# Reordering the first loads and widening the first six steps of a fused window-attention and feed-forward kernel

## The chip, the core and the metric

The kernel runs on one core of one Trainium2 chip. The metric is the device time of one execution in microseconds; the kernel before takes 308.42 us (median of three runs, 308.12 to 308.52). The profiler's record of one execution spans 306.1 us. The engines are TensorE (PE: matmuls; PEld: its weight loads), VectorE (DVE), ScalarE (ACT), GpSimd (POOL, which here mostly issues loads) and SyncE (SP, which issues the output's stores).

## What is computed

Sliding-window attention over 8 batches, 8 heads, 576 positions and head size 64, where a position sees those up to 32 away, and then a two-layer feed-forward network over the 4608 tokens with a smooth ReLU between the layers:

```python
scores = q @ k.T / sqrt(64); outside |i - j| <= 32: -1e9
x      = softmax(scores) @ v                 # (4608, 512) after the heads are put side by side
h      = x @ w_in                            # w_in  (512, 2048)
g      = h where h >= 1, 0 where h <= -1, (h + 1)**2 / 4 between
out    = g @ w_out                           # w_out (2048, 512)
```

Inputs and output are fp32. The loads cast to bf16 on their way, but for the first half of the first batch's q, which comes as fp32 (`q32`) and is cast on the core. Matmuls take bf16 and sum in fp32.

## The kernel before

**Units of work.** The first layer is cut into slots. Slot `a` is token block `t = a // 8` of 256 tokens and feature block `f = a % 8` of 256 features: eight matmuls of 256 columns into `hp` (128 x 512 fp32, one bank of PSUM). The smooth ReLU of a slot is an ACT step and two DVE steps, or, for the slots in `two_on_act`, two ACT steps and one DVE step:

```python
A.activation(rr, hp, AF.Relu, scale=0.5, bias=0.5)
if a in two_on_act:
    A.activation(mx, rr, AF.Square)
    V.scalar_tensor_tensor(g, hp, 1.0, mx, op0=ALU.max, op1=ALU.min)
else:
    V.tensor_max(mx, hp, rr)
    V.scalar_tensor_tensor(g, rr, 1.0, mx, op0=ALU.min, op1=ALU.mult)
```

Attention of a batch is cut into: `tpose` (q or k is transposed by PE, and copied out of PSUM by ACT and DVE), `scores` (a mask matmul by `add_mask` while slots are below 14, the products, Exp on ACT), `sums` (products with v and with ones into one tile; its `end` takes Ln and Exp on ACT for the reciprocal and puts off a DVE product into `xT`, which `flush()` issues), and `scores8` for the last 96 positions. The rows `kk = 0, 2` of `xT` come from `sums` with `y1 = 0`, and `kk = 1, 3` from `y1 = 1`.

The second layer's first two token blocks go in `pair(x)`: eight matmuls of 256 columns, with `half = x // 8` the half of w_out's columns, `p = x % 8 // 4` the token block, and `x % 4` the group of four of w_out's 16 row groups. They accumulate in a tile of `ps_o`:

```python
pairs = [(6, 0), (7, 1), (8, 2), (9, 3), (11, 4), (12, 5), (15, 6), (15, 8), (16, 7), (17, 9)]   # (slot, pair)
```

**Loads.** GpSimd issues them in this order (`load_half(1, ...)` is the rest of the first batch's q and k, `load_rows(1, ...)` the second batch's q and k):

```python
for h in range(2):
    load_half(0, 1, h)               # k of the first half
load_v(0, 0) ... load_v(0, 3)
cuts = [0, 256, 512, 768, 1024, 1280, 1792, DFF]
w = [(load_w_in, c0, c1, h) for c0, c1 in zip(cuts, cuts[1:]) for h in range(2)]
put(w[:4] + [(load_half, 1, t, h) for t in range(2) for h in range(2)] + w[4:12])
put([(load_w_out, 0, 0, 4)] + w[12:])
put([(load_w_out, 0, k, k + 4) for k in range(4, 16, 4)] + [(load_rows, 1, t) for t in range(2)])
put([(load_v, 1, n) for n in range(4)])
```

**The start.** PSUM has pools `ps_h` (two tiles of one bank), `ps_s` and `ps_n` (one tile of two banks each) and, for the start, `ps_p` (two banks), whose place `ps_o` (two tiles of one bank) takes later. `keep_warm(n, ...)` issues n matmuls on a tile of zeros, whose result is not used.

```python
    ...                                   # q and k of the first half: transposes, copies, scores
    keep_warm(4, ps_h, "hp")
    e0 = sums(0, 0, 0, TB)
    e1 = sums(0, 1, 0, TB, ps_p)
    keep_warm(5, ps_h, "hp")
    e0()
    e1()
```

**The slots.** What is to happen at a slot is in a list by `at`; a slot's matmuls and its smooth ReLU come first, then what `at` holds for it, then its pairs, then what `at` holds for the slot and a half.

```python
at(1, (tposes, 0, (0, 1), (1, 1)))                                      # the rest of q and k
at(2, (scores, 0, (0, 1), (0, 2), (2, 4)), (scores8, 0, ps_o))
at(3, (scores, 0, (1, 2), (0, 2), (2, 4), ps_n), (sums, 0, 0, TB, MAIN, ps_s))
at(4, (sums, 0, 1, TB, MAIN))
at(5, (sums, 0, 0, MAIN, S, ps_s))
at(13, seq[0][1])                                                       # second batch: scores
at(13.5, (*seq[1][1], ps_n))
at(14, (*seq[0][0], ps_s), seq[1][0])                                   # second batch: sums
for t in range(2):
    at(11 + t, (tposes, 1, (t, 0), (t, 1)))                             # second batch: q, then k
```

From slot 18 on the kernel goes on in the same manner, with the loads of later batches well ahead, and none of that is touched by the change.

Of the kernel before, what the change touches and what calls it, by code (L numbers as in the profile page):

```python
# [14 lines left out]
def kernel(  # L15
# [29 lines left out]
    WIDE = 72, 136  # L45
    LONG = 2

    const = ctx.enter_context(tc.tile_pool(name="const", bufs=1))
# [5 lines left out]
    osp = ctx.enter_context(tc.tile_pool(name="osp", bufs=3))  # L54
    ps_h = ctx.enter_context(tc.tile_pool(name="ps_h", bufs=2, space=bass.MemoryType.PSUM))
    ps_s = ctx.enter_context(tc.tile_pool(name="ps_s", bufs=1, space=bass.MemoryType.PSUM))
# [24 lines left out]
    def load_half(half, t, h, eng=None, x=None):  # L81

        src, dst, nm = ((q, qn, "qh"), (k, kn, "kh"))[t]
        if (0, half) not in dst:
            dst[0, half] = early.tile([128, 2, S], BF, name=nm, tag=nm, bufs=2) if x is None else x
        (eng or nc.gpsimd).dma_start(out=dst[0, half][:, h], in_=src[0].rearrange(  # L86
            "(h y) (l p j) d -> h l p y (j d)", h=2, l=2, p=32)[h][half])
# [21 lines left out]

    def load_w_in(c0, c1, h):  # L110
        nc.gpsimd.dma_start(out=w_in[64 * h:64 * h + 64, :, c0:c1],  # L111
                            in_=moe_w_in.rearrange("(h y d) f -> h d y f", h=2, d=64)[h][:, :, c0:c1])

# [33 lines left out]

    cuts = [0, 256, 512, 768, 1024, 1280, 1792, DFF]
    w = [(load_w_in, c0, c1, h) for c0, c1 in zip(cuts, cuts[1:]) for h in range(2)]
    put(w[:4] + [(load_half, 1, t, h) for t in range(2) for h in range(2)] + w[4:12])  # L150
    put([(load_w_out, 0, 0, 4)] + w[12:])
    put([(load_w_out, 0, k, k + 4) for k in range(4, 16, 4)] + [(load_rows, 1, t) for t in range(2)])
    put([(load_v, 1, n) for n in range(4)])
# [85 lines left out]

    def scores8(b, eng, pool=None):  # L240

        p = pt8[b] = ptp.tile([128, 2, 2, TAIL], BF, name="pt8")
        if pool:
            ps = [pool.tile([128, 2 * TAIL], FP, name="s8", tag="op") for h in range(2)]
        else:
            bb = two_banks(ps_s)
            ps = [bb[:, h, :2 * TAIL] for h in range(2)]
        if eng is None:
            add_mask(ps, 2, TAIL)
        for y1 in range(2):  # L250
            for a in range(2):
                for h in range(2):
                    s0 = S * (y1 + 2 * a) + MAIN
                    nc.tensor.matmul(ps[h][HD[a], TAIL * y1:TAIL * y1 + TAIL], kT[b][HD[h], s0 + 32:s0 + TAIL],
                                     qTs[b % 3][HD[h], PAD + s0:PAD + s0 + TAIL],
                                     start=eng is not None, stop=True, skip_group_check=True)
        like = "p h y j -> p h (y j)"
        if pool:
            for h in range(2):
                A.activation(p[:, h].rearrange("p y j -> p (y j)"), ps[h], AF.Exp, scale=D ** -0.5)  # L260
        else:
            A.activation(p.rearrange(like), bb[:, :, :2 * TAIL], AF.Exp, scale=D ** -0.5)
        mask(eng, p, mask8.rearrange("p (h y j) -> p h y j", h=2, y=2))
# [55 lines left out]

    def tp1(pool):  # L320
        if pool is ps_h:
            return pool.tile([128, 8, 128], BF, name="tp", tag="hp")
        return pool.tile([128, 2, 8, 128], BF, name="tp", tag="bb")[:, 0]

    def tposes(b, *sets):

        todo = []
        for (t, half), pool in zip(sets, (ps_s, ps_n)):
            tp = pool.tile([128, 2, 8, 128], BF, name="tp", tag="bb")
            todo += [tpose(b, 2 * half + part, t, (A.copy, V.tensor_copy)[part], tp[:, part]) for part in range(2)]  # L330
        for copy in todo:
            copy()

    def keep_warm(n, pool, tag):

        z = pool.tile([128, 512], FP, name="z", tag=tag)
        for _ in range(n):
            nc.tensor.matmul(z, warm[:, :128], warm, start=True, stop=True)

# [7 lines left out]

    with tc.tile_pool(name="ps_p", bufs=1, space=bass.MemoryType.PSUM) as ps_p:
        keep_warm(11, ps_h, "hp")

# [4 lines left out]
        qn[0, 0] = cast(q32, "qb", 5)  # L355
        qq = [tpose(0, n, 0, (A.copy, V.tensor_copy)[n], tp1(ps_h)) for n in range(2)]
        for x in qq:
            x()
        kk = [tpose(0, n, 1, (A.copy, V.tensor_copy)[n], tp1((ps_n, ps_p)[n])) for n in range(2)]
        keep_warm(1, ps_h, "hp")  # L360
        first = two_banks(ps_s)
        add_mask([first[:, h] for h in range(2)], 4, 128)
        for x in kk:
# [3 lines left out]
        scores(0, (1, 2), (0, 2), (0, 2), None, ps_p)  # L367
        keep_warm(4, ps_h, "hp")
        e0 = sums(0, 0, 0, TB)
        e1 = sums(0, 1, 0, TB, ps_p)  # L370
        keep_warm(5, ps_h, "hp")
        e0()
        e1()
    ps_o = ctx.enter_context(tc.tile_pool(name="ps_o", bufs=2, space=bass.MemoryType.PSUM))

    NB = NT // TB
    NF = DFF // 256  # L380
    pairs = [(6, 0), (7, 1), (8, 2), (9, 3), (11, 4), (12, 5), (15, 6), (15, 8), (16, 7), (17, 9)]
    two_on_act = (1, 7, 8, 9, 10, 11, 12)
    ev = {}
# [12 lines left out]

    at(1, (tposes, 0, (0, 1), (1, 1)))
    at(2, (scores, 0, (0, 1), (0, 2), (2, 4)), (scores8, 0, ps_o))
    at(3, (scores, 0, (1, 2), (0, 2), (2, 4), ps_n), (sums, 0, 0, TB, MAIN, ps_s))
    at(4, (sums, 0, 1, TB, MAIN))  # L400
    at(5, (sums, 0, 0, MAIN, S, ps_s))
    seq = [x for b in range(1, B) for x in steps(b, 224)]
    at(13, seq[0][1])
    at(13.5, (*seq[1][1], ps_n))
    at(14, (*seq[0][0], ps_s), seq[1][0])
# [9 lines left out]
    for t in range(2):  # L415
        at(11 + t, (tposes, 1, (t, 0), (t, 1)))
    loads, xps = {}, {16: [(2, 0)], 18: [(2, 1)]}
# [55 lines left out]
    def run(pos):  # L473
        todo = []
        for fn, *x in ev.get(pos, []):
            if fn is sums:
                todo.append(sums(*x))
            elif fn is tposes:
                tposes(*x)
            else:  # L480
                pool = (x.pop(),) if x[-1] in (ps_s, ps_n, ps_o) else ()
                fn(*x, eng, *pool)
        for end in todo:
            end()

    def project(hp, f, r0, todo, first, last):

        for n, (j, kk) in enumerate(todo):
            nc.tensor.matmul(hp[:, j], w_in[:, kk, 256 * f + 128 * j:256 * f + 128 * j + 128],  # L489
                             xT[:, kk, r0:r0 + TB], start=first and n == 0, stop=last and n == len(todo) - 1,  # L490
                             skip_group_check=True)

    hps = []
    done = 4 * (40 - NF)
    for a in range(NF * NB + 2 * NF):
        wide = WIDE[0] <= a < WIDE[1]
        eng = None if a < 14 else V
        post = [] if a >= 40 else [x for n, x in pairs if n == a] + [a - NF] * (a >= 2 * NF + 2)
        for b, x in loads.get(a, []):
            if x < 2:  # L500
                load_nat(b, x)
            else:
                for n in range(4):
                    load_v(b, n)
        if a == 0 or a > 3:
            flush()
        if a < NF * NB:
            if wide:
# [3 lines left out]
                hp = ps_h.tile([128, 2, TB], FP, name="hp", tag="hp")  # L512
                for n, kk in enumerate((0, 2, 1, 3)):
                    nc.tensor.matmul(hp.rearrange("p n t -> p (n t)"), w_in[:, kk, 128 * f:128 * f + 128],  # L514
                                     xT[:, kk, r0:r0 + 2 * TB], start=n == 0, stop=n == 3)
                g = gT[:, f, home(t):home(t + 1) + 1:home(t + 1) - home(t)]
            else:
                t, f = divmod(a, NF)
                r0 = TB * t % RING
                if a in (0,):  # L520
                    hps = [ps_h.tile([128, 2, TB], FP, name="hp", tag="hp") for _ in range(2)]
                    for y in range(2):
                        for n in range(2):
                            project(hps[n], f + n, r0, [(j, y + 2 * m) for j in range(2) for m in range(2)], y == 0, y == 1)
                elif not hps:
                    pool, tag = (ps_o, "op") if a == 6 else (ps_h, "hp")
                    hps = [pool.tile([128, 2, TB], FP, name="hp", tag=tag)]
                    project(hps[0], f, r0, [(j, kk) for j in range(2) for kk in (0, 2, 1, 3)], True, True)
                hp = hps.pop(0)
                g = gT[:, 2 * f:2 * f + 2, home(t)]  # L530

            rr = ewp.tile([128, 2, TB], FP, name="rr")
            A.activation(rr, hp, AF.Relu, scale=0.5, bias=0.5)  # L533
            mx = ewp.tile([128, 2, TB], FP, name="mx")
            if a in two_on_act:
                A.activation(mx, rr, AF.Square)
                V.scalar_tensor_tensor(g, hp, 1.0, mx, op0=ALU.max, op1=ALU.min)
            else:
                V.tensor_max(mx, hp, rr)  # L539
                V.scalar_tensor_tensor(g, rr, 1.0, mx, op0=ALU.min, op1=ALU.mult)  # L540
        flush()
# [45 lines left out]
```

The softmax here doesn't subtract the row's maximum and nothing guards it: scores larger than these inputs give would overflow.

## Time and profile before

| | before |
|---|---|
| time, median of 3 | 308.42 us |
| span of the profiled execution | 306.1 us |
| granted TensorE clock | 1.00 |
| moved by DMA | 35.67 MB, mean 117 GB/s |
| HBM read, written | 36.70 MB, 9.44 MB |

A line of the timeline reads: start in us, busy us, engine, source line, operation, output <- inputs, shape and count, and in brackets the idle time of the engine before it with what ended it. In the windows view a line has the stretch, its length, and for PE, PEld, DVE, ACT and POOL the busy time and number of instructions, then the granted clock, the busy time of the DMA engines as a share (their packets overlap, so it passes 1), and GB/s. Line 489 is a slot's first-layer matmul, line 464 a pair, line 189 a transpose of q or k, lines 539, 540 and 537 the DVE steps of a slot, and line 307 the product into `xT`.

### The profile page before, as it was taken

The page shows a single profiled execution, that of the slowest core. Times are in us where ns is not written, and L with a number is a line of the kernel's source. Part 1 is how long each engine was busy: PE and PEld are TensorE (multiplying, and loading weights), DVE is VectorE, ACT ScalarE, POOL GpSimd, SP SyncE. Part 2 cuts the span into 40 slices and gives each one's busy share as a digit, 9 for nine tenths or more (in the row PEclk, how much of TensorE's full clock was granted, in tenths as well). Part 3 has the DMA queues.
Part 4 walks back from the last instruction along what each step waited for, and adds up shares of the span by engine and source line. Part 5 has one row for each costly group of instructions (what it writes and reads, how often), then busy time and mean ns, then how long its engine had stood idle before and what let it go on. Part 6 is the DMA issues. An engine that isn't in the chain of part 4 may idle for free.

```text
span 306.1 us, 7974 instructions
## 1 busy us (share of the span) xinstructions
PE 298.4 (97%) x3388; PEld 181.2 (59%) x3388; DVE 239.6 (78%) x376; ACT 191.2 (62%) x320; POOL 77.1 (25%) x92
## 2 busy tenths in 40 slices
PE   8889999999999999999999999999999999999995
PEld 3468878876666676666654544444445444446644
DVE  3268568888888989998999998888888888788700
ACT  3688896748856856776766766665667654444311
POOL 8787661037009009004600900000000000000000
PEclk9999999999999999999999999999999999999999
DMA  9999999999999999999998991550101000000121
GB/s 153 184 197 198 186 196 153 173 156 164 139 186 109 181 169 124 165 144 116 148 127 166 145 156 39 111 115 34 36 34 37 36 34 35 36 34 34 59 80 69
DMA packets 137171, 35.67 MB, mean 117 GB/s; under 512 B 122160, under 2 KB 132912, under 8 KB 137136
## 3 DMA queue, kind: packets, MB, share of 16 engines
q0 software_dynamic: 102976, 18.06, 83.5%
q1 hardware_dynamic: 34016, 16.81, 26.1%
q8 instruction: 26, 0.43, 0.6%
q10 hardware_dynamic: 144, 0.29, 0.3%
q14 instruction: 9, 0.07, 0.1%
HBM read 36.70 MB, written 9.44 MB: 151 GB/s over the span
## 4 chain that ended last, share of the span: by engine, by line
PE 91%; POOL 3%; DMA 2%; ACT 1%; issue 1%; DVE 0%; POOLq 0%; ACTq 0%
PE op L449 36%; PE hp L489 22%; PE hp L514 18%; PE bb L295 6%; PE op L464 4%; PE bb L229 2%; DMA w_in<-in_moe_w_in_dram 2%; POOL vn L107 1%; PE op L440 1%; POOL w_in L111 1%; PE tp L189 1%; ACT pt L237 1%; POOL kh L86 1%; POOL qh L86 0%; PE bb L208 0%
## 5 line engine op out<-in xcount | busy, mean ns | idle before, releaser
L533 ACT ACTIVATE rr<-hp 128x512 f32<-128x512 f32 x144 | 85.5, 595 | 86.1 <-PE hp L514 41.7
L449 PE MATMUL op<-w_out,gT 128*128 128x512 bf16 x496 | 126.9, 380 | 0.0
L539 DVE TENSOR_TENSOR mx<-hp,rr 128x512 f32<-128x512 f32 x137 | 94.4, 689 | 26.1 <-ACT rr L533 24.3
L540 DVE SCALAR_TENSOR_TENSOR gT<-rr,mx 128x512 bf16<-128x512 f32 x137 | 94.8, 692 | 4.7
L489 PE MATMUL hp<-xT,w_in 128*128 128x256 bf16 x640 | 83.1, 273 | 2.2 <-DMA w_in<-in_moe_w_in_dram 1.4
L489 PEld LDWEIGHTS <-w_in 128*128 128x128 bf16 x640 | 61.8, 98 | 22.7 <-issue 2.8
L449 PEld LDWEIGHTS <-gT 128*128 128x128 bf16 x496 | 46.1, 98 | 45.2
L514 PE MATMUL hp<-xT,w_in 128*128 128x512 bf16 x256 | 65.7, 379 | 0.0
L514 PEld LDWEIGHTS <-w_in 128*128 128x128 bf16 x256 | 25.0, 98 | 30.2
L99 POOL DMA_DIRECT2D qn<-in_q_dram x12 | 14.6, 1224 | 89.5 <-DMA kT<-kn 87.4
L237 ACT ACTIVATE pt<-bb 128x1024 bf16<-128x1024 f32 (+1 forms) x33 | 32.7, 1001 | 4.5 <-PE bb L229 3.1
L107 POOL DMA_DIRECT2D vn<-in_v_dram x32 | 27.7, 900 | 4.8 <-DMA w_out<-in_moe_w_out_dram 4.0
L307 DVE TENSOR_TENSOR xT<-bb,rc 128x512 bf16<-128x512 f32 (+1 forms) x32 | 21.0, 657 | 9.6 <-ACT rc L302 8.7
L453 ACT COPY osb<-op 128x512 f32<-128x512 f32 x31 | 18.0, 580 | 11.4 <-PE op L449 11.1
L302 ACT ACTIVATE rc<-lr 128x512 f32<-128x512 f32 (+2 forms) x40 | 23.5, 587 | 1.3
L301 ACT ACTIVATE lr<-bb 128x512 f32<-128x512 f32 (+2 forms) x40 | 22.1, 552 | 0.3 <-PE bb L295 0.3
L203 DVE TENSOR_TENSOR pt<-pt,mask 128x1024 bf16<-128x1024 bf16 (+1 forms) x33 | 20.3, 614 | 0.5 <-ACT pt L237 0.5
L295 PE MATMUL bb<-pt,ones 64*64 64x256 bf16 (+3 forms) x352 | 19.6, 255 | 0.1
L295 PE MATMUL bb<-pt,vn 64*64 64x128 bf16 (+3 forms) x712 | 18.4, 204 | 0.1
L295 PEld LDWEIGHTS <-ones 64*64 64x64 bf16 x352 | 10.3, 105 | 11.6 <-issue 11.6
L295 PEld LDWEIGHTS <-vn 64*64 64x64 bf16 x712 | 16.7, 107 | 0.3 <-DMA vn<-in_v_dram 0.3
L464 PE MATMUL op<-w_out,gT 128*128 128x256 bf16 x128 | 16.5, 273 | 0.0
(61 smaller groups left out, 140.3 us busy)
## 6 DMA issues: line engine op xcount, KB each, us to landing
out_dram<-osb SPq DMA_DIRECT2D x35, 256.0 KB, 2.3
vn<-in_v_dram POOLq DMA_DIRECT2D x32, 144.0 KB, 9.7
qn<-in_q_dram POOLq DMA_DIRECT2D x12, 288.0 KB, 6.2
kn<-in_k_dram POOLq DMA_DIRECT2D x12, 288.0 KB, 9.0
w_in<-in_moe_w_in_dram POOLq DMA_DIRECT2D x12, 128.0 KB, 5.6
w_out<-in_moe_w_out_dram POOLq DMA_DIRECT2D x4, 256.0 KB, 8.0
w_out<-in_moe_w_out_dram POOLq DMA_DIRECT2D x2, 512.0 KB, 13.2
kh<-in_k_dram POOLq DMA_DIRECT2D x4, 144.0 KB, 5.4
```

The lines of the kernel that those rows point to most:

```text
L107: nc.gpsimd.dma_start(out=vn[b][64 * a:64 * a + 64, :, h], in_=v[b, y:y + 2].rearrange("y s d -> (y s) d") .rearrange("(c r) d -> r c d", ...
L237: A.activation(p, ps[:, :, :w * n].rearrange(like, y=m), AF.Exp, scale=D ** -0.5)
L295: nc.tensor.matmul(bb[HD[h], a, o + c0:o + c1], ones[HD[a]] if c is None else vn[b][HD[a], c, h], p(a, h), start=n == 0, stop=True, skip_g ...
L301: A.activation(lr[:, :, :D0], bb[:, :, D0:2 * D0], AF.Ln)
L302: A.activation(rc[:, :, :D0], lr[:, :, :D0], AF.Exp, scale=-1.0)
L449: nc.tensor.matmul(op[tt], gT[:, j, home(tt // 2), 128 * (tt % 2):128 * (tt % 2) + 128], w_out[:, j], start=j == 0, stop=j == 15)
L464: nc.tensor.matmul(o[:, tt], gT[:, j, p, 128 * tt:128 * tt + 128], w_out[:, j, 256 * half:256 * half + 256], start=not done, stop=len(done ...
L489: nc.tensor.matmul(hp[:, j], w_in[:, kk, 256 * f + 128 * j:256 * f + 128 * j + 128], xT[:, kk, r0:r0 + TB], start=first and n == 0, stop=l ...
L514: nc.tensor.matmul(hp.rearrange("p n t -> p (n t)"), w_in[:, kk, 128 * f:128 * f + 128], xT[:, kk, r0:r0 + 2 * TB], start=n == 0, stop=n == 3)
L533: A.activation(rr, hp, AF.Relu, scale=0.5, bias=0.5)
L539: V.tensor_max(mx, hp, rr)
L540: V.scalar_tensor_tensor(g, rr, 1.0, mx, op0=ALU.min, op1=ALU.mult)
```

## The change

It does five things. The rest of the first batch's q and k is loaded ahead of w_in. w_in comes in pieces of 512 columns and of every second row group `kk` (0 and 2, or 1 and 3), each in two halves of the partitions, where it came in pieces of 256 columns and all row groups. The first batch's whole attention is done by the start section, woven between slots 0 to 5, which are now three `double` steps: two slots in one tile of two banks, whose ReLU steps have 1024 columns. The second batch's q and k are loaded ahead of half of w_out's first columns, and transposed at slots 10 and 11, between the slot's ACT steps and its DVE step. And the pairs, the choice of `two_on_act` and the PSUM tiles of slots 6 to 8 are set anew. It is for fewer waits of TensorE at the start. The core of the diff:

```diff
-    cuts = [0, 256, 512, 768, 1024, 1280, 1792, DFF]
-    w = [(load_w_in, c0, c1, h) for c0, c1 in zip(cuts, cuts[1:]) for h in range(2)]
-    put(w[:4] + [(load_half, 1, t, h) for t in range(2) for h in range(2)] + w[4:12])
-    put([(load_w_out, 0, 0, 4)] + w[12:])
-    put([(load_w_out, 0, k, k + 4) for k in range(4, 16, 4)] + [(load_rows, 1, t) for t in range(2)])
+    put([(load_half, 1, t, h) for t in range(2) for h in range(2)])
+    put([(load_w_in, c, e, h) for c in range(0, DFF, 512) for e in range(2) for h in range(2)])
+    put([(load_w_out, 0, k, k + 4) for k in (0, 4)] + [(load_rows, 1, t) for t in range(2)])
+    put([(load_w_out, 0, k, k + 4) for k in (8, 12)])
 ...
+    def smelu(hp, g, rr, mx, two_on_act, mid=None):
+        A.activation(rr, hp, AF.Relu, scale=0.5, bias=0.5)
+        if two_on_act:
+            A.activation(mx, rr, AF.Square)
+            flush()
+            if mid:
+                mid()
+            V.scalar_tensor_tensor(g, hp, 1.0, mx, op0=ALU.max, op1=ALU.min)
+        else:
+            flush()
+            V.tensor_max(mx, hp, rr)
+            V.scalar_tensor_tensor(g, rr, 1.0, mx, op0=ALU.min, op1=ALU.mult)
 ...
+    def double(n, pool, between=None):
+        hp = pool.tile([128, 2, 2, TB], FP, name="hp4", tag="bb")
+        for kk in KK:                                            # 0, 2, 1, 3
+            for f in range(2):
+                project(hp[:, f], 2 * n + f, 0, [(j, kk) for j in range(2)], kk == KK[0], kk == KK[-1])
+            if kk == KK[1] and between:
+                between()
+        smelu(hp.rearrange("p n j t -> p (n j t)"), gT[:, 4 * n:4 * n + 4, 0], rr4[n % 2], mx4, False)
 ...
-        keep_warm(5, ps_h, "hp")
+        tp = tp2(ps_e)
+        qq = [tpose(0, 2 + n, 0, (V.tensor_copy, A.copy)[n], tp[:, n]) for n in range(2)]
         e0()
+        flush()
+        qq[0]()
         e1()
+        flush()
+        qq[1]()
+        keep_warm(3, ps_n)
+        tp = tp2(ps_s)
+        kk = [tpose(0, 2 + n, 1, (V.tensor_copy, A.copy)[n], tp[:, n]) for n in range(2)]
+        rest = two_banks(ps_n)
+        add_mask([rest[:, h] for h in range(2)], 4, 128)
+        for x in kk:
+            x()
+        scores(0, (0, 1), (0, 2), (2, 4), None, ready=rest)
+        double(0, ps_e, lambda: scores(0, (1, 2), (0, 2), (2, 4), None))
+        sums(0, 0, TB, MAIN)()
+        scores8(0, None)
+        double(1, ps_p)
+        sums(0, 1, TB, MAIN, ps_s)()
+        double(2, ps_e, lambda: sums(0, 0, MAIN, S)())
 ...
-    pairs = [(6, 0), (7, 1), (8, 2), (9, 3), (11, 4), (12, 5), (15, 6), (15, 8), (16, 7), (17, 9)]
-    two_on_act = (1, 7, 8, 9, 10, 11, 12)
+    pairs = [(8, 0), (9, 1), (11, 4), (12, 2), (13, 5), (14, 3), (15, 6), (15, 8), (16, 7), (17, 9)]
+    two_on_act = (6, 7, 8, 9, 10, 11, 12)
 ...
-    at(13, seq[0][1])
-    at(13.5, (*seq[1][1], ps_n))
+    at(12.5, seq[0][1])
+    at(13, (*seq[1][1], ps_n))
 ...
-        at(11 + t, (tposes, 1, (t, 0), (t, 1)))
+        at(10.25 + t, (tposes, 1, (t, 0), (t, 1)))
 ...
+                if a == 8:
+                    hp = two_banks(ps_s)[:, 0].rearrange("p (j t) -> p j t", j=2)
+                else:
+                    pool, tag = (ps_o, "op") if a < 8 else (ps_h, "hp")
+                    hp = pool.tile([128, 2, TB], FP, name="hp", tag=tag)
+            smelu(hp, g, rr, mx, a in two_on_act, lambda: run(a + 0.25))
```

At the start `ps_e` (two banks) takes the place of `ps_h`, which is opened after it, together with `ps_o`.

## The prediction

> **What bounds the kernel now.** I read the page first, then the windows view cut at the points where the work changes, then TensorE's waits, then the timelines of the first 45 us. The page:
>
> ```profile
> span 306.1 us, 7974 instructions
> PE 298.4 (97%) x3388; PEld 181.2 (59%) x3388; DVE 239.6 (78%) x376; ACT 191.2 (62%) x320; POOL 77.1 (25%) x92
> ```
>
> TensorE (PE) is busy 97% of the span; nothing else is over 78%. Where the other 3% lie is told by the windows view (busy time in each stretch):
>
> ```profile
> 0.00:11.60 11.60, 10.11 (x152) 5.24 (x153) 3.34 (x16) 5.80 (x8) 10.26 (x20) 1.00 1.50 158
> 11.60:33.60 22.00, 19.29 (x301) 15.08 (x299) 14.85 (x23) 17.35 (x32) 17.31 (x25) 1.00 1.34 199
> 33.60:44.80 11.20, 11.05 (x216) 8.87 (x216) 6.95 (x11) 9.88 (x16) 7.11 (x7) 1.00 1.83 189
> 44.80:302.80 258.00, 257.93 (x2726) 152.05 (x2724) 214.45 (x327) 157.84 (x266) 42.39 (x42) 1.00 1.05 105
> ```
>
> The second number is the length, the third PE's busy time. After 44.8 us PE has 0.07 us of idle time in 258 us, and the change leaves that work alone. So the whole effect must show before that point, which is the first-layer product of slot 15. The change can move the end only by the time at which PE finishes slot 15. What could be won is the idle time from 11.6 to 44.8 us, 2.71 + 0.15 = 2.9 us, some 0.2 us more for each wait (a matmul's recorded end is later than the next one's issue: 8 of them start 0.87 us apart, the last ends at 1.04), and the filler matmuls on `warm`: 4 to 5 us, 1.5% of the span. A gain of 2% is out of reach. PE's timeline names the waits:
>
> ```profile
> 13.24 0.60 PE L489 MATMUL hp<-xT,w_in 128*128 128x256 bf16 x4 [0.44 <-DVE xT L307]
> 14.50 1.47 PE L489 MATMUL hp<-xT,w_in 128*128 128x256 bf16 x12 [0.67 <-DMA w_in<-in_moe_w_in_dram]
> ...
> 17.12 0.69 PE L189 MATMUL tp<-ident,kh 128*64 128x128 bf16 x17 [0.47 <-DMA kh<-in_k_dram]
> 18.53 1.03 PE L489 MATMUL hp<-xT,w_in 128*128 128x256 bf16 x8 [0.72 <-DMA w_in<-in_moe_w_in_dram]
> 33.59 1.03 PE L489 MATMUL hp<-xT,w_in 128*128 128x256 bf16 x8 [0.33 <-DVE gT L537]
> ```
>
> Three are for loads. DVE's timeline shows the other engine that matters; here it works off slots 4 and 5 without a gap, and ends only at 27.9 us:
>
> ```profile
> 24.68 0.68 DVE L539 TENSOR_TENSOR mx<-hp,rr 128x512 f32<-128x512 f32 x1
> 25.39 0.69 DVE L540 SCALAR_TENSOR_TENSOR gT<-rr,mx 128x512 bf16<-128x512 f32 x1
> 26.00 0.62 DVE L307 TENSOR_TENSOR xT<-bb,rc 128x448 bf16<-128x448 f32 x1
> 26.54 0.68 DVE L539 TENSOR_TENSOR mx<-hp,rr 128x512 f32<-128x512 f32 x1
> 27.25 0.69 DVE L540 SCALAR_TENSOR_TENSOR gT<-rr,mx 128x512 bf16<-128x512 f32 x1
> ```
>
> [...]the trace has 688 for line 539. [...]2 x 0.61 when two of 512 follow each other without a gap (29.04 to 29.65). [...]before, w_in's packets are 512 B, mostly, and move 192 to 198 KB/us, q and k at 1152 B some 204, v at 128 B 135 to 162. Packets of 1024 B will thus gain a few per cent at most. [...]the granted clock is 1.00 in every window.
>
> **The change part by part, loads first.** The page's DMA row is 9 in all early slices: loads come at the rate of the DMA engines, so order is all. A landing is an issue (GpSimd timeline) plus the time to landing (DMA view). Before: the fourth piece of v at 10.6, the fourth of w_in 14.4, the last k half 17.1, and from there 128 KB of w_in each 0.65 us. After, the q and k halves (144 KB, 0.7 us each) follow v: 11.4, 12.1, 12.85 and, with half a microsecond for the slow spot near 13 us, 13.9. w_in comes then in 16 pieces of 128 KB. By the same sum of bytes the first 512 columns are complete at 17.1, their even row groups at 15.75; the later quarters at 19.75, 22.45, 25.15. Then w_out's first two quarters 26.5 and 27.85, q and k of the second batch 30.8 and 33.7 (before: 33.3 and 36.2), w_out's others 35.1 and 36.5.
>
> **Then PE's new order,** with issue times from the timeline: 8 matmuls of 256 columns 0.875, an 18-transpose half of q or k 0.56, mask and scores 0.34 + 0.22, sums 0.42 to 0.53; 0.2 from the last issue to ACT's start, 0.05 from DVE to PE. In the instruction order of the built kernel a second copy out of a shared transpose tile waits for the first, on the other engine; I keep that.
>
> The sums end at 11.54 as before. q's transposes wait for 12.2 (0.66 lost), the fillers for DVE's product until 13.23 (0.47), k's for 14.0 (0.13); the mask ends 14.9. k's copies, DVE 0.75 then ACT 0.65, end at 15.97: scores at 16.02 (1.12 lost). Slots 0 and 1 are multiplied 16.24 to 18.56, with scores between. ACT: Exp to 18.95, 1024-column Relu (estimated 1.03 from the Exp of that width) to 19.9. On PE the sums and tail scores follow, slots 2 and 3 to 20.97, a wait of 0.5 for the tail's Exp, sums, slots 4 and 5 to 24.32.
>
> DVE now begins its first slot at 19.9, against 16.2 before, and from there it is full: six steps of 1024 at 1.24, two products of 0.62 and one of 0.55 make 9.2 less overlap, so to 28.85; slot 6's step ends 29.5. PE waits 0.7 for the last quarter of w_in, does slots 6, 7, 8 to 27.66, and then meets the first pair. That needs an accumulator from the pool `ps_o` of two buffers, and slots 6 and 7 hold both. It waits for slot 6's step: 29.53, 1.87 lost. Then pair 0, slot 9, pair 1, slot 10 to 33.03, q's 36 transposes, slot 11 to 35.02. k's transposes follow with nothing between but slot 11, and share q's two buffers: they wait for q's copies on ACT and DVE until 35.97 and 36.65 (1.07 lost; before, a pair and a slot lay between). Pair 4, slot 12, pair 2, scores, slot 13, scores, pair 5, slot 14, sums, pair 3, slot 15: 9.3 us with no wait, to 46.5.
>
> Sum: 0.66 + 0.47 + 0.13 + 1.12 + 0.5 + 0.14 + 0.7 + 1.87 + 1.07 = 6.7 us lost where the kernel before loses 4 to 5, two fillers saved included. Slot 15 ends at 46.5 instead of 44.8: +1.7 us, 310.1.
>
> **Rivals.** *Loads were the bound, and the order mends it.* For it: the three longest of these waits are for w_in and k. If DVE keeps up, so that neither the pair nor k's transposes wait, 2.9 of the 6.7 us go: 307.2. Against: DVE has over nine microseconds queued after 19.9. *A new bound on DVE, held through `ps_o`:* my main reading, 309 to 311. *Late loads:* a slow spot in k's landing shifts everything after 14 us one for one, up to +1 us: 311. *Clock:* [...]I give it 3%.
>
> **Range and chances.** My sum of waits has an error of perhaps 1 us either way; a slot order so deliberately rearranged (pairs 2 and 3 put off, slot 8 in `ps_s`) speaks for fewer waits than I count, so I shade down by half a microsecond: 309.6 us, 307.6 to 311.4 for 8 in 10. Faster by over 2% (below 302.3) would need more than all idle time: 0.01. Slower by over 2% (above 314.6) needs a stall I don't see: 0.02. Within 2%: 0.97.
>
> **What would show it.** Right: PE's record of the first pair has some 1.5 us idle before it, released by DVE's gT step; the first matmuls on w_in start near 16.2 and wait for no load; slot 6 waits under 1 us for w_in; k's second-batch transposes wait 1 us for a copy; PE from slot 15 on has no gaps. Wrong: the first pair starts without a wait near 27.7 (the wide steps are shorter or begin earlier than I hold), or slot 15 ends before 44.8.

## The result and the profile after

| | before | after |
|---|---|---|
| time, median | 308.40 us (308.12 to 308.52, 4 executions) | 312.12 us (310.58 to 312.43, 4 executions) |
| span of the profiled execution | 306.1 us | 308.8 us |
| TensorE ends slot 15 there | 44.8 us | 47.5 us |

The ratio is 1.0107, with a 95% interval of 1.0072 to 1.0142: the change makes the kernel 1.1% slower. The predicted 309.6 us and its range (to 311.4) lie below the median. The six executions on record, two of them beside these four, fall into two kinds, which the median hides: two with a granted TensorE clock of 1.000 take 310.44 and 310.58 us, and four with 0.994 or 0.995 take 312.02 to 312.43. The profiled one is of the first kind. So there are two things to explain, 2.2 us that every execution has and 1.7 us that most have.

The windows view of after, cut at the same work as before (start to end, length, then busy time of PE, PEld, DVE, ACT, POOL, then clock):

```profile
0.00:11.60 11.60, 9.41 (x146) 4.68 (x150) 3.81 (x16) 5.58 (x8) 9.66 (x19) 1.00 1.48 158
11.60:33.60 22.00, 17.52 (x296) 13.55 (x282) 13.36 (x16) 16.61 (x26) 18.76 (x28) 1.00 1.25 198
33.60:47.40 13.80, 13.16 (x238) 10.67 (x236) 8.41 (x13) 11.14 (x19) 8.96 (x9) 1.00 2.12 175
47.40:305.40 258.00, 257.92 (x2727) 152.30 (x2724) 213.54 (x326) 157.59 (x265) 41.26 (x40) 1.00 1.03 104
```

The last row is that of before, 258 us with 0.08 us idle, moved by 2.6 us. The time was lost ahead of it: TensorE is idle for 2.2 us in the first row against 1.5 (0.55 of it a wait for v), 4.5 in the second against 2.7, and 0.6 in the third against 0.15. What TensorE waits for, in the waits view of after (total, times, longest):

```profile
PE op L504 <- DVE gT L353: 2.0, 1, 2.0
PE bb L229 <- ACT kT L192: 1.3, 1, 1.3
...
PE bb L328 <- DVE xT L299: 0.8, 1, 0.8
PE tp L189 <- DVE qT L192: 0.6, 1, 0.6
PE bb L287 <- DMA vn<-in_v_dram: 0.6, 1, 0.6
```

Before, this list had 1.4 us for w_in (two waits) and 0.5 for k. No wait for w_in is left: the loads do what they were moved for. The waits are now for the other engines, and are longer. In PE's timeline (L341 is the first layer, L504 a pair, L189 a transpose, L229 scores):

```profile
16.99 0.42 PE L229 MATMUL bb<-qT,kT 64*64 64x128 bf16 x16 [1.32 <-ACT kT L192]
17.34 1.05 PE L341 MATMUL hp<-xT,w_in 128*128 128x256 bf16 x8
...
27.48 1.03 PE L341 MATMUL bb<-xT,w_in 128*128 128x256 bf16 x8 [0.18 <-DVE xT L302]
30.50 1.03 PE L504 MATMUL op<-w_out,gT 128*128 128x256 bf16 x8 [1.98 <-DVE gT L353]
...
36.90 1.34 PE L189 MATMUL tp<-ident,kn 128*64 128x128 bf16 x36 [0.64 <-DVE qT L192]
```

And DVE's timeline of the same stretch:

```profile
21.02 1.23 DVE L356 TENSOR_TENSOR pt<-hp,rr 128x1024 f32<-128x1024 f32 x1 [4.83 <-ACT rr L347]
22.28 1.23 DVE L357 SCALAR_TENSOR_TENSOR gT<-rr,pt 128x1024 bf16<-128x1024 f32 x1
...
28.59 1.25 DVE L357 SCALAR_TENSOR_TENSOR gT<-rr,pt 128x1024 bf16<-128x1024 f32 x1
29.77 1.27 DVE L353 SCALAR_TENSOR_TENSOR gT<-hp,mx 128x512 bf16<-128x512 f32 x2
```

DVE stands idle for 4.83 us up to 21.0, then works without a gap to slot 6's step at 30.4, and at once the first pair starts on TensorE. This is the chain that was predicted, one microsecond later than predicted. That the lateness is handed on along it is what two of the runs below test.

### The profile page after: what moved, and what is told of

It reads as the page before. It is cut to its first block, busy times and chain, and to the rows that moved or that the text cites. A ratio compares the mean times of both kernels' runs of the same rounds, so it can differ in the third digit from the quotient of the medians.

```text
span 308.8 us, 7959 instructions
## 1 busy us (share of the span) xinstructions
PE 298.0 (97%) x3386; PEld 181.2 (59%) x3386; DVE 239.1 (77%) x370; ACT 191.3 (62%) x316; POOL 78.6 (25%) x94
## 4 chain that ended last, share of the span: by engine, by line
PE 89%; DVE 2%; DMA 2%; POOL 2%; issue 2%; ACT 2%; POOLq 0%; DVEq 0%; ACTq 0%
PE op L489 36%; PE hp L341 20%; PE hp L545 18%; PE bb L287 6%; PE op L504 5%; PE bb L229 2%; DMA kh<-in_k_dram 2%; DVE pt L356 1%; PE op L480 1%; POOL vn L107 1%; PE tp L189 1%; ACT rr L347 1%; POOL kh L86 0%; POOL qh L86 0%; ACT pt L237 0%
## 5 line engine op out<-in xcount | busy, mean ns | idle before, releaser
L347 ACT ACTIVATE rr<-hp 128x512 f32<-128x512 f32 (+1 forms) x139 | 83.4, 601 | 85.5 <-PE hp L341 42.7
L356 DVE TENSOR_TENSOR mx<-hp,rr 128x512 f32<-128x512 f32 x131 | 90.3, 689 | 24.2 <-ACT rr L347 22.4
L357 DVE SCALAR_TENSOR_TENSOR gT<-rr,mx 128x512 bf16<-128x512 f32 x131 | 90.6, 692 | 4.5
L341 PE MATMUL hp<-xT,w_in 128*128 128x256 bf16 x632 | 81.5, 273 | 0.0
L341 PEld LDWEIGHTS <-w_in 128*128 128x128 bf16 x640 | 61.9, 98 | 19.9 <-issue 0.8
L99 POOL DMA_DIRECT2D qn<-in_q_dram x12 | 14.6, 1222 | 91.5 <-DMA kT<-kn 90.7
L504 PE MATMUL op<-w_out,gT 128*128 128x256 bf16 x128 | 16.5, 273 | 2.0 <-DVE gT L353 2.0
```

The costliest lines, as they stand in the source:

```text
L504: nc.tensor.matmul(o[:, tt], gT[:, j, p, 128 * tt:128 * tt + 128], w_out[:, j, 256 * half:256 * half + 256], start=not done, stop=len(done ...
```

## The experiments

Theory A: every execution loses the waits seen above, which come from a late start of the scores, passed on by a full DVE through the two buffers of `ps_o`. Theory B: in most executions TensorE's clock is also lowered for a few microseconds (a mean of 0.994 or 0.995), as a consequence of a wait. Rivals: chance of the chip, loads, or waits that come back elsewhere when one is removed. The figures "at full clock" are from executions with a clock of 0.998 or more.

**Again.** The changed kernel, unaltered.

> The changed kernel once more, unaltered, for the spread of its time and of its granted clock. Theory A (the added time has two parts: 2.7 us of waits that every execution has, and a lowered TensorE clock for some 3 us in those executions whose granted clock is 0.995): most executions at 312.0 to 312.5 us with a clock near 0.995, some at 310.4 to 310.7 with 1.000, nothing between. Rival (312 was a chance of that chip): all near 310.5.

Six executions: 310.50 and 310.67 at 1.000, and 312.07 to 312.34 at 0.994 to 0.995; ratio 1.0125 (1.0109 to 1.0140). Two kinds again, and nothing between. Nine executions of the kernel before, on the same chip, all had 0.999 or 1.000.

**Fillers**, 18 matmuls on zeros in three of the waits:

```diff
+        keep_warm(3, ps_s)
         keep_warm(3, ps_n)
 ...
         add_mask([rest[:, h] for h in range(2)], 4, 128)
+        keep_warm(6, ps_p)
 ...
         run(a)
+        if a == 8:
+            keep_warm(9, ps_n)
```

> The changed kernel with 18 matmuls on zeros put into three of its waits on TensorE (3 ahead of the fillers before k's transposes, 6 between the mask and the scores, 9 between slot 8 and the first pair), each wait long enough to hold them. If TensorE's idle time is what lowers its clock: every execution at a clock of 1.000 and 310.4 to 310.8 us, 1.6 us less than the changed kernel's usual time. If the lowered clock has another cause (load of the chip, other engines): the same mix of 310.5 and 312.2 as without them.

Five executions, 310.53 to 310.86, clock 0.998 to 1.000; ratio to before 1.0075 (1.0063 to 1.0088). Work was added, and the median fell from 312.13 to 310.72. So TensorE's idle time lowers its clock (to 0.994 or 0.995 in eight of twelve executions without the fillers, in none of five with them). Which idle time, the next two tell.

**Fill late** (the nine before the first pair alone) and **fill early** (the other nine alone).

> The changed kernel with nine matmuls on zeros between slot 8 and the first pair, and nothing else altered. All the fillers together kept the clock at 1.000. Theory L (the 2 us wait ahead of the first pair is what lowers the clock): all executions 310.4 to 310.9 us at 1.000. Theory E (it is the idle stretch from 12.7 to 17 us): most executions still at 312.0 to 312.5 with 0.995.

> The changed kernel with nine matmuls on zeros in the waits before 17 us (3 ahead of the fillers before k's transposes, 6 between mask and scores), and none before the first pair. Theory L: most executions still at 312.0 to 312.5 with a clock of 0.995. Theory E: all at 310.4 to 310.9 with 1.000. If neither of this run and its sister is free of the lowered clock, both stretches count.

Fill late: five of six executions at 310.43 to 310.83 and full clock, one at 312.45 with 0.995. Fill early: four of five at 312.21 to 312.36 with 0.994 to 0.995, one at 310.65. The wait ahead of the first pair is the main cause; the early stretch can hardly do it alone (one in six). The profile of fill early is of an execution with a lowered clock. Its windows, cut at the two recorded changes of the clock (31.30 and 34.71 us) and in steps of 3.41 us from there:

```profile
24.47:27.89 3.42, 3.25 (x43) 2.72 (x32) 3.39 (x5) 3.25 (x7) 3.20 (x5) 1.00 1.33 201
27.89:31.30 3.41, 1.45 (x14) 1.15 (x13) 3.38 (x5) 2.16 (x4) 3.31 (x4) 1.00 1.22 208
31.30:34.71 3.41, 3.41 (x19) 2.43 (x17) 0.39 (x2) 1.23 (x2) 2.00 (x3) 0.50 1.45 192
34.71:38.10 3.39, 3.21 (x54) 2.58 (x53) 0.95 (x2) 2.22 (x4) 2.41 (x2) 1.00 2.67 152
```

In the second row TensorE is busy for 1.45 us of 3.41, because it waits for DVE ahead of the pair:

```profile
30.49 1.13 PE L506 MATMUL op<-w_out,gT 128*128 128x256 bf16 x8 [1.96 <-DVE gT L353]
```

In the third, and in that alone, the clock is 0.50, while TensorE is fully busy. 3.41 us at 0.50 cost 1.7 us: the distance between the two kinds. In the profile of after, at full clock, the edge between two windows of that length (counted in steps of 3.413 us from its recorded change at 5.23 us) cuts the wait:

```profile
25.70:29.12 3.42, 2.64 (x23) 2.06 (x22) 3.39 (x5) 3.36 (x7) 3.13 (x6) 1.00 1.27 207
29.12:32.53 3.41, 2.03 (x19) 1.82 (x19) 2.52 (x4) 1.03 (x3) 2.96 (x3) 1.00 1.23 203
```

TensorE is busy for 2.64 and 2.03 us of the two, and the clock stays.

**Two tiles.** ACT's and DVE's copies of k came out of one PSUM tile. In after, DVE's copy starts at 15.36, when all 18 transposes are done, and ACT's at 16.22, when DVE's is.

```diff
-        tp = tp2(ps_s)
-        kk = [tpose(0, 2 + n, 1, (V.tensor_copy, A.copy)[n], tp[:, n]) for n in range(2)]
+        tp = [tp2(ps_s)[:, 0], tp2(ps_p)[:, 0]]
+        kk = [tpose(0, 2 + n, 1, (V.tensor_copy, A.copy)[n], tp[n]) for n in range(2)]
```

> The changed kernel with the two halves of k's transposes in two PSUM tiles of their own, so that ACT's copy needn't wait for DVE's. Theory (the late start of slots 0 to 5 is passed on through DVE to the first pair and the end): scores start at 16.25 instead of 16.99, the first pair 0.75 us earlier, and the span is 308.0 to 308.2 at a clock of 1.000. Rival (the loads of w_in hold the slots, or the pair is held by something else): scores earlier, end unchanged at 308.8.

```profile
16.16 0.42 PE L229 MATMUL bb<-qT,kT 64*64 64x128 bf16 x16 [0.47 <-ACT kT L192]
...
29.65 1.03 PE L504 MATMUL op<-w_out,gT 128*128 128x256 bf16 x8 [1.96 <-DVE gT L353]
```

DVE's copy now starts at 15.16 and ACT's at 15.39. The scores start 0.83 us earlier, the first pair 0.85, and the span at full clock is 307.9, 0.9 to 1.0 less. The late start is passed on in full: theory A. The wait before the pair stays at 1.96, and so does the lowered clock (0.994 in three of four executions).

**Square.** One DVE step fewer ahead of slot 6: `rr4[n % 2], mx4, False` in `double` becomes `rr4[n % 2], mx4, n == 2`.

> The changed kernel with one thing altered: slots 4 and 5 take their square on ACT, so that DVE has one 1024-column step fewer ahead of slot 6 (1.23 us). Theory (DVE's backlog holds slot 6's accumulator and so the first pair): the wait ahead of the first pair falls from 1.98 to 1.0 us (ACT's 1.0 us square takes back some 0.3), span 307.8 to 308.0 at a clock of 1.000. Rival (the pair waits for w_out or for ACT): wait and span unchanged, or longer by ACT's 1.0 us.

```profile
29.80 1.03 PE L504 MATMUL op<-w_out,gT 128*128 128x256 bf16 x8 [1.15 <-DVE gT L353]
```

The wait is 1.15, the span 308.0 to 308.2, so 0.6 to 0.8 us less, somewhat under the 0.8 to 1.0 expected. That shows DVE's backlog as what holds the pair. And only one of four executions has the lowered clock, 0.994.

**K later.** k of the second batch after slot 11's pair: `at(10.25 + t, ...)` becomes `at((10.25, 11.5)[t], ...)`.

> The changed kernel with the second batch's k transposed after slot 11's pair and not between slot 11's ACT and DVE steps. Theory (k's transposes wait for the copies of q out of the same two buffers, 0.64 us, and this time is lost): the wait goes and the span is 308.2 at a clock of 1.000. Rival (what is gained is lost again before slot 15, as k's copies or the scores come later): span 308.7 to 308.9, with a new wait ahead of the scores.

The wait ahead of these transposes is gone, and none takes its place before slot 15. One execution at full clock took 309.75, 0.8 us less than after; the three others (0.992 to 0.994) took 311.43 to 311.79, 0.5 to 0.8 less than after's of that kind at their median (312.25 of eight, with again).

**Narrow.** The wide steps undone:

```diff
-        smelu(hp.rearrange("p n j t -> p (n j t)"), gT[:, 4 * n:4 * n + 4, 0], rr4[n % 2], mx4, False)
+        for i in range(2):
+            smelu(hp[:, i].rearrange("p j t -> p (j t)"), gT[:, 4 * n + 2 * i:4 * n + 2 * i + 2, 0],
+                  rr4[n % 2][:, 512 * i:512 * i + 512], mx4[:, 512 * i:512 * i + 512], False)
```

> The changed kernel with each 1024-column ReLU step of slots 0 to 5 cut into two of 512 columns again (slot by slot: Relu, max, min-times), matmuls and order left. The 1024-column step was estimated at 1.24 us and measured at 1.23; two of 512 start 0.61 to 0.72 us apart. Theory (DVE is full from its first step to slot 6's, so that what counts is its sum: 4 x 0.68 against 2 x 1.23 is 0.25 us more in each of three pairs, less 0.4 us by which the first step begins earlier): first pair 0.3 us later, span 309.1 at a clock of 1.000. Rival (the wide step's later start is the dearer): first pair 0.3 to 0.4 us earlier, span 308.4.

A miss for both: 313.54 us, ratio 1.0168 (1.0153 to 1.0183), the first pair at 32.44 after a wait of 2.86 us, and all four executions with a lowered clock, 0.995. 0.6 us of the pair's 1.94 us was there already when the scores started (17.59). The rest shows on ACT:

```profile
20.56 0.60 ACT L347 ACTIVATE rr<-hp 128x512 f32<-128x512 f32 x1
21.92 0.60 ACT L347 ACTIVATE rr<-hp 128x512 f32<-128x512 f32 x1 [0.76 <-DVE pt L356]
```

ACT's second Relu waits 0.76 us for DVE's read of the first, in each of the three pairs, and everything behind it on ACT is late (the sums of the first batch wait 0.9 us more). Both slots lie in one PSUM tile of two banks, where each had a tile of its own in the kernel before. They share the tile of `rr4` too, and no run parts the two; that a wait of this sort went in two tiles, where PSUM alone was parted (ACT's copy began 0.23 us after DVE's there, 0.86 us after it in after), speaks for PSUM. So the run does not price the width alone; it shows that here, where two slots share their tiles, the cut step lost these three waits of 0.76 us.

**Q and k of the second batch late**, in the changed kernel and in the version named best below: the four loads of w_out's first columns in one run, and `load_rows` behind them, as before.

> The changed kernel with the second batch's q and k loaded after all of w_out's first columns again, as before the change. If this part of the change does nothing as things stand (TensorE comes to these transposes only at 34.1 and 36.9 us, and they would land near 33.0 and 35.7 even so): span 308.7 to 309.0 at a clock of 1.000, no new wait. Rival (the early load is needed): a wait ahead of q's transposes, span up by 0.5 us or more.

> The version with the four waits removed, and the second batch's q and k loaded after all of w_out's first columns again. There TensorE comes to q's transposes at 32.1 us and to k's at 35.1. If these loads land near 33.0 and 35.7, then a wait of 0.9 us ahead of q's shows, and the span is 306.6 to 306.9 instead of 305.9: this part of the change is worth something only once the waits ahead of it are gone. If not: 305.9.

In the changed kernel: 310.36 and 310.71 at full clock, no new wait. That part of the change does nothing there. In the best version:

```profile
33.16 1.20 PE L188 MATMUL tp<-ident,qn 128*64 128x128 bf16 x36 [1.30 <-DMA qn<-in_q_dram]
```

A wait of 1.30 us for q, where 0.9 was expected (q landed at 33.1 as expected; TensorE came at 31.9, not at 32.1), and a span of 307.0 in the profile, 1.1 us more. The profiled execution is the fastest of eleven. Their median, 309.50, is 1.9 us above the best version's; what the other 0.8 us are is open.

**Loads only.** The kernel before with the change's order and pieces of q, k and w_in, and none of its order of work.

> The kernel before with the change's order and pieces of q, k and w_in, and its own order of work (w_out and the second batch as before). Slots 0 and 1 come ahead of the rest of q and k in that kernel, so they now wait for w_in's first 512 columns until 15.6 (even rows) and 16.9 (odd rows) where they went on at 14.5: theory (the order of loads pays only with attention drawn ahead of the slots): TensorE idle for about 3 us before 15.6, slots 0 and 1 done at 17.9 instead of 15.9, span 308 to 309 (1.5 to 2.5 us up). Rival (the rest of q and k was the true hold of the start): span 306.0 or less.

```profile
15.64 1.03 PE L487 MATMUL hp<-xT,w_in 128*128 128x256 bf16 x8 [2.77 <-DMA w_in<-in_moe_w_in_dram]
```

The wait for w_in is there, 2.77 us. The two executions at full clock span 307.8 and 308.9, 1.1 and 2.2 us over the kernel before as it ran beside them (306.7 at the median of fourteen), where 1.5 to 2.5 were expected; ratio 1.0068 (1.0045 to 1.0092). The clock is lowered here too, to 0.994 in two of four: in the profiled one it is 0.50 from 16.86 to 20.27 us, behind the wait. So the new order of loads costs time in the old order of work. The attention drawn ahead of the slots with the loads in their old order was not run, so what the new order of loads is worth there is not shown.

**Best.** Four waits removed at once: two tiles, square and k later as above, and the first two pairs both after slot 9 (`pairs = [(9, 0), (9, 1), ...`), so that slot 9 runs while DVE finishes.

> The changed kernel with four things altered: two PSUM tiles for k's halves, slots 4 and 5 with their square on ACT, the first two pairs both after slot 9 (so that slot 9 fills the wait ahead of the first pair), and k of the second batch after slot 11's pair. If the waits found so far are what the change costs and they add up (0.9, 0.8, 0.7 and 0.6 us): span 305.8 to 306.2, time 307.5 to 308.0, under the kernel before by 0.2%, and a clock of 1.000 throughout as no wait over 1.2 us is left. Rival (a wait removed comes back at the next stage): 308.5 to 309.5.

307.63 us (307.35 to 307.74, seven executions, clock 0.998 to 1.000); ratio to before 0.9974 (0.9963 to 0.9984). The version beats the kernel before by 0.26%, and the change as it was by 1.4%. PE's timeline:

```profile
16.45 0.42 PE L229 MATMUL bb<-qT,kT 64*64 64x128 bf16 x16 [0.47 <-ACT kT L192]
...
28.52 1.03 PE L341 MATMUL hp<-xT,w_in 128*128 128x256 bf16 x8 [0.53 <-DVE gT L353]
29.39 1.91 PE L504 MATMUL op<-w_out,gT 128*128 128x256 bf16 x16
```

The 1.98 us before the pair are 0.53 before slot 9, and the pairs wait for nothing. The span is 2.9 us below the 308.8 of after. Two tiles, square and k later took off 0.9, 0.7 and 0.8 us by themselves; the new place of the first pair was not run alone, and the 0.5 us left for it is a difference, not a measurement.

## Why the prediction was wrong, point by point

| step | predicted | measured after |
|---|---|---|
| last half of k lands | 13.9 us | 14.6 us |
| scores of the rest start, after a wait of | 16.02, 1.12 us | 16.99, 1.32 us |
| first 1024-column step on DVE | 19.9 us | 21.0 us |
| such a step takes | 1.24 us | 1.23 us |
| slot 6's step ends | 29.5 us | 30.4 us |
| wait ahead of the first pair | 1.87 us | 1.98 us |
| wait of slot 6 for w_in | 0.7 us | none |
| wait ahead of k's second-batch transposes | 1.07 us | 0.64 us, then slower |
| slot 15 ends | 46.5 us | 47.5 us |
| clock | 1.000, 3% for less | lowered in 8 of 12 executions |

*What bounds the kernel, and where the change can act:* right. All of the difference lies ahead of the end of slot 15, and the 258 us behind it are unchanged.

*The mechanism at full clock:* right. DVE's row of wide steps holds slot 6's buffer and so the first pair; square and two tiles show both ends of that chain. The 1.24 us of a wide step was the author's estimate; the second of two steps of 512 columns starts 0.61 us after the first in before (29.04 to 29.65), and the wide step took 1.23. *Its size:* short by one microsecond in slot 15's end, all of it there by the start of the scores. The terms: k landed 0.7 later than allowed for, so that its transposes went on only at 14.63 and DVE's copy began 0.8 late, at 15.36; and k's copies took 0.83 and 0.71 us, where 0.75 and 0.65 were used, as the wider of them now is DVE's. (v's last piece also came 0.27 us later than in the profile before, 10.89 against 10.62, and put DVE's products back by 0.3, but the wait for k covers that.) From there the sum carried on with nearly the right intervals to the end. That slot 6 found w_in landed follows from the delay, and w_in's last piece came at 24.67, before the 25.15 of the sum. Against the median of before, which is above its profiled execution, the waits are worth 2.2 us, where the sum had 1.7.

*The shading* by half a microsecond, for an order "so deliberately rearranged", had nothing in the profile behind it, and made the miss larger.

*The rival "Clock":* this is the step that failed. Its 3% rested on an estimate of the author's that no trace of before could bear out. A wait of 1.96 us was enough where enough of it fell inside one window of 3.41 us: in k later and fill early, which both waited so long ahead of the pair, TensorE was busy for 1.29 and 1.45 us of a window, and the next one ran at 0.50. It adds 1.7 us to most executions, and this puts the median out of the range: 308.4 + 2.2 + 1.7 = 312.3. That the same kernel shows both kinds would fit windows that lie differently in each execution: the clock's first recorded change is at 5.23 us in after and at 5.63 in again, so windows of 3.41 us counted from there cut the same work at other places. Nor is "1.00 in every window" right for the first microseconds: the profile of before has no record of the clock up to 6.48 us, which the windows view shows as 1.00, but the fillers of 512 columns start 0.43 us apart there, and 0.21 to 0.23 us apart from 9.2 us on.

*The other rivals:* late loads were part of it (0.7 us of k). That the order of the loads would mend the start was wrong at TensorE and right at the queue: no wait for w_in is left, and those for engines cost more.

## What to carry to other kernels

When loads are put in a better order, follow the work behind them engine by engine: the time went to one engine that started late (DVE, at 21.0 us) and then had ten microseconds without a gap, and to a buffer that this engine held. An idle stretch of 1.96 us on TensorE cost another 1.7 us by the clock in fill early, nearly twice its length in all, so put work, or even matmuls on zeros, into such a stretch (fill late: 310.63 us at the median, against 312.13). And two engines that read one PSUM tile by parts were made to wait for one another here (ACT's copy of k began 0.86 us after DVE's, and 0.23 with two tiles): try a tile of its own for each part.

## What the runs showed of the hardware

- Recorded stretches of one clock last 3.41 (at 0.50 in fill early, k later, narrow and loads only), 10.24 (loads only), 23.89 (k later) and 27.31 us (narrow, fill early), which is 1, 3, 7 and 8 times 3.41: as far as these runs show, the clock changes at the edges of windows of that length. After windows in which TensorE was busy for 0.55 us (narrow), 1.03 (loads only), 1.29 (k later) and 1.45 us (fill early) the next one ran at 0.50; after windows with 1.75 (q and k of the second batch late, in the changed kernel), 1.82 (square, early), 2.03 (after) and 2.31 us (again) it ran at 1.00. By busy time as the profile models it, up to 43% of the window went with the one and 51% or more with the other in these runs.
- The window at 0.50 followed the idle one in these four runs, so its cost fell on work that has nothing to do with the wait. In k later it is that of 30.87 to 34.28 us:

```profile
27.46:30.87 3.41, 1.29 (x11) 1.00 (x11) 3.38 (x5) 2.71 (x5) 2.54 (x4) 1.00 1.21 208
30.87:34.28 3.41, 3.41 (x19) 2.43 (x17) 0.89 (x2) 0.26 (x1) 1.95 (x4) 0.50 1.34 200
```

- In before, after and loads only the load that is under way near 13 us lands 1.9 to 2.0 us after the one ahead of it, whatever it carries (w_in in the first, k in the others), where 0.7 us is usual. In each one packet of 16 KB of instructions starts at 12.1 to 12.5 us. That it is the cause was not tested, and against it, another such packet at 19.98 us in after left the next landings 0.62 to 0.70 us apart.
- w_in's pieces with packets of 1024 bytes landed 0.65 us apart for 128 KB, against 0.61 to 0.79 with 512 bytes: nothing gained that counts.
